# First mixture with one slot for each expert, up to 384 token columns wide, and weights split in halves

## The chip, the core and the metric

The kernel runs on one core of a Trainium2 chip. A core has a matrix engine (PE, with PEld for its weight loads), a vector engine (DVE), a scalar engine (ACT), GpSimd (POOL) and SyncE (SP), which mostly issues DMAs; 16 DMA engines move data between DRAM and the on-chip memories, SBUF and PSUM (8 banks, written by PE). The metric is device time for one execution in microseconds, lower is better.

## The reference

Three layers one after the other, on 1792 tokens of 768 values; what matters here is the second.

```python
# 1. attention: 4 batches, 12 heads, 448 positions, 64 wide, with heads mixed before and after softmax
# 2. first mixture: 8 experts, D = 768, F = 1024; each token goes to one expert
    logits = x @ w_gate
    expert_idx = np.argmax(logits, axis=1)
    ...
    for e in range(E):
        mask = expert_idx == e
        xe = x[mask]
        h = np.maximum(xe @ w1[e], 0.0)
        ye = h @ w2[e]
        out[mask] = gate_w[mask, None] * ye
# 3. second mixture, dense: 768 -> 2048 -> 768
    h = x @ w_in
    r = np.maximum(h, 0.0)
    return ((r * r) @ w_out).astype(np.float32)
```

With the reference's inputs the experts 0 to 7 get 448, 22, 11, 302, 376, 116, 157 and 360 tokens. All are float32; the second mixture's weights come as float64.

## The kernel before

**Precision.** Every float32 operand is split in a high part (fp32r) and the rest, and a product is three matmuls: high by high, high by low, low by high. For a weight tile, `split` (L1021) lets ACT cast the high part (L1042) and DVE, or for a few tiles POOL, subtract the low part (L1043). `ahead` keeps six such tiles made (WB = 6), so a step's tile is made five steps before PE needs it. ACT's and DVE's instructions stand in the order in which the code calls them.

**Router.** During attention, `Router` counts tokens by expert in units of 128 (TM). `early` picks two units for slot 0 before all tokens are known; `table` gives the units of the rest their places, while PE works on slot 0. `side` in `emit_all` steps through this, once per `half` step of slot 0 (PH says at which). After that `ready` is set and the waiting weight reloads and gathers are issued.

**First mixture.** SLOTS has 6 doubles (256 tokens, one expert) and 6 singles (128) in turn, 18 units. A slot loads its expert's w1 (6 tiles of 128 x 1024, `raw1`) and w2 (8 tiles of 128 x 768, `raw2`) by `reload`, on SP's queue, as soon as the slot before has split the same tile. In a double (`double1` L1082, `double2` L1113) the weights are PE's stationary operand and 256 token columns move; the output stands transposed, and `drelu` and `dput` evict it. In a single (`stage1` L1143, `stage2` L1175) the tokens are stationary and 512 or 256 weight columns move; `htrans` and `ytrans` transpose its hidden layer and its result. `xtrans` transposes gathered tokens on PE. The order on PE is pairwise: stage 1 of the double, stage 1 of the single, stage 2 of the double, stage 2 of the single. If a routing needs more units than the 18, `tc.If(more < NT)` runs four more singles and a further piece of the second mixture.

**Conversion.** `convert` turns the float64 w_out to float32 in between: 18 tasks of 7 DVE instructions (`Conv.parts`, L914 to L922), `next(conv)` a part. After a task ACT issues the load of a later one (`conv_load`, into `craw`, CR = 3 buffers), and SP stores the result. `CD` says how many parts follow each step of a double. `compact1` scatters each token's place to DRAM, 16 times, 4 bytes a token (`cid`).

**Second mixture.** `ysplit` makes the operand of 512 tokens, `st1` (L1277) and `st2` (L1316, L1318) alternate for 64 rounds. `open2` opens its pools within the last slot.

Of the kernel before, what the change touches and what calls it, by code (L numbers as in the profile page):

```python
# [7 lines left out]
F32 = mybir.dt.float32  # L8
# [8 lines left out]
DM = H * D  # L17
# [475 lines left out]
QP = QS = 6  # L493
# [9 lines left out]
XK = ((4,6),(3,5))  # L503
CD = (2,2,2,2,2,2),(2,2,2,2,2,2,1,1)
PH = (3,4,5,6,7,8,9,9,10,12,13)
# [3 lines left out]
XS = 3  # L509
HK = 5  # L510
HL = 3
A2 = -1
XD = 12
C0 = 6
W2 = (0,0,1,1,2,2,3,3)
PD = (2,),(2,5)
PS = (2,),(2,5)
# [5 lines left out]
class Router:  # L523

# [51 lines left out]

# [30 lines left out]
    def fill2(self):  # L607
# [4 lines left out]

        self.mate = p.tile([NB, NB], F32, name="mate")
        yield G.memset(self.mate, 1.0)
        yield G.affine_select(out=self.mate, in_=self.mate, compare_op=ALU.is_ge, fill=0.0, base=0,
                              pattern=[[-2, NB // 2], [0, 2]], channel_multiplier=1)
        yield G.affine_select(out=self.mate, in_=self.mate, compare_op=ALU.is_ge, fill=0.0, base=1,
                              pattern=[[2, NB // 2], [0, 2]], channel_multiplier=-1)
# [4 lines left out]
        yield V.tensor_scalar_mul(cst[:, 7:8], cst[:, 6:7], float(TM))  # L623

        self.late = p.tile([UMAX, 1], F32, name="late")
        n = UMAX // 3 - 1
        li = p.tile([UMAX, n], I32, name="li")
        yield G.iota(li, pattern=[[-3, n]], base=0, channel_multiplier=1)
        lt = p.tile([UMAX, n], F32, name="lt")
        yield V.tensor_copy(lt, li)  # L630
        yield V.tensor_scalar(lt[:, 0:1], self.cc[0:UMAX], float(URUN), None, ALU.is_ge)
        yield V.tensor_scalar(lt[:, 1:], lt[:, 1:], 2.0, None, ALU.is_equal)
        yield V.tensor_reduce(self.late, lt, axis=AX.X, op=ALU.max)
# [86 lines left out]
    def units(self, u0, u1, new_ps, tbi):  # L720
# [8 lines left out]
        for z in range(2):  # L729
            nc.tensor.matmul(ps[0:u1, 67 + z:68 + z], lhsT=self.sel[:, z:z + u1], rhs=self.cst[:, 4:5], start=True, stop=True)  # L730
# [4 lines left out]
        V.tensor_copy(tb[:, 0:5], ps[0:u1, 64:69])  # L735
        V.tensor_copy(tbi[:, 0:1], tb[:, 0:1])
        V.scalar_tensor_tensor(out=tb[:, 5:6], in0=tb[:, 4:5], scalar=tb[:, 3:4], in1=self.late[0:u1], op0=ALU.subtract, op1=ALU.mult)
        V.tensor_tensor(out=tb[:, 5:6], in0=tb[:, 5:6], in1=tb[:, 3:4], op=ALU.add)
        V.tensor_tensor(out=tb[:, 6:7], in0=tb[:, 0:1], in1=tb[:, 2:3], op=ALU.add)
        V.scalar_tensor_tensor(out=tbi[:, 2:3], in0=tb[:, 6:7], scalar=tb[:, 5:6], in1=tb[:, 2:3],  # L740
                               op0=ALU.not_equal, op1=ALU.mult)

    def early(self, new_ps):
# [27 lines left out]
        ps = new_ps()  # L771
        nc.tensor.matmul(ps[0:NB, 0:1], lhsT=self.mate, rhs=sel[:, 2:3], start=True, stop=True)
        yield

        V.tensor_scalar(col[:, 2:3], ps[0:NB, 0:1], -1.0, 1.0, ALU.mult, ALU.add)
        yield PE
        yield from self.units(0, EARLY, new_ps, self.tbe)

    def table(self, new_ps):
# [3 lines left out]
        odd, even = cst[:, 5:6], cst[:, 6:7]  # L783
        x = [col[:, i:i + 1] for i in range(16)]
        yield PE
        ps = new_ps()
        self.counts(ps)
        yield

        V.tensor_scalar(x[0], ps[0:NB, 0:1], cst[:, 3:4], None, ALU.subtract)  # L790
        V.tensor_scalar(x[4], x[0], cst[:, 7:8], x[2], ALU.is_gt, ALU.mult)
        V.tensor_tensor(out=x[5], in0=x[4], in1=even, op=ALU.mult)
        V.scalar_tensor_tensor(out=x[6], in0=x[0], scalar=0.0, in1=x[3], op0=ALU.is_gt, op1=ALU.subtract)
        V.tensor_scalar(cst[:, 1:2], x[0], 0.0, float(TM), ALU.max, ALU.min)
        yield PE
        ps = new_ps()
        nc.tensor.matmul(ps[0:NB, 0:1], lhsT=tri, rhs=x[5], start=True, stop=True)
        yield

        V.tensor_scalar(x[7], ps[0:NB, 0:1], odd, None, ALU.subtract)  # L800
        V.tensor_scalar(x[4], x[7], float(QP - 1), x[4], ALU.is_lt, ALU.mult)
        V.tensor_tensor(out=x[5], in0=x[4], in1=even, op=ALU.mult)
        V.tensor_tensor(out=x[6], in0=x[6], in1=x[4], op=ALU.subtract)
        V.tensor_scalar(x[7], x[7], 3.0, odd, ALU.mult, ALU.add)
# [3 lines left out]
        nc.tensor.matmul(ps[0:NB, 1:2], lhsT=ones, rhs=x[5], start=True, stop=True)  # L808
        yield


        Q, fr = x[8], x[9]
        V.tensor_copy(Q, ps[0:NB, 0:1])
        V.tensor_scalar(fr, ps[0:NB, 1:2], -1.0, float(QP - 1), ALU.mult, ALU.add)
        V.scalar_tensor_tensor(out=x[10], in0=Q, scalar=float(QS), in1=fr, op0=ALU.is_ge, op1=ALU.mult)
        V.scalar_tensor_tensor(out=x[11], in0=Q, scalar=-float(QS), in1=fr, op0=ALU.add, op1=ALU.is_lt)
        V.scalar_tensor_tensor(out=x[11], in0=Q, scalar=float(QS), in1=x[11], op0=ALU.is_ge, op1=ALU.mult)
        V.tensor_tensor(out=x[12], in0=Q, in1=fr, op=ALU.subtract)
        V.tensor_scalar(x[12], x[12], 2.0, -2.0 * QP - 1, ALU.mult, ALU.add)
# [105 lines left out]
class Moe:  # L925

    WB, NA = 6, 1

    def __init__(self, tc, ctx, rt, cv, w1, w2, ident, out, slots, main):
# [803 lines left out]
```

## Time and profile before

| | |
|---|---|
| median of 3 runs | 1469.14 us (1465.86 to 1483.52) |
| profiled execution | 1476.49 us, span of its instructions 1474.8 us |
| PE busy | 1383.5 us (94%) |
| DVE busy | 1048.0 us (71%) |
| ACT, POOL busy | 819.7 us (56%), 479.3 us (32%) |
| DMA | 276.49 MB, 187 GB/s in the mean |

A profile shows one execution. "Busy" is the time in which an engine worked on instructions; PE's matmuls overlap, and how fast they follow each other is read from their starts. The chain of waits is followed back from the last instruction: at each step to what released it. A stretch table gives busy time by engine, the granted TensorE clock (PEclk, 1.00 is 2.4 GHz), the DMA engines' busy share and their rate. Times count from the span's start: attention to about 630 us, the first mixture to 987, the second to the end.

### The profile page before, as it was taken

The page shows a single profiled execution, that of the slowest core. Times are in us where ns is not written, and L with a number is a line of the kernel's source. Part 1 is how long each engine was busy: PE and PEld are TensorE (multiplying, and loading weights), DVE is VectorE, ACT ScalarE, POOL GpSimd, SP SyncE. Part 2 cuts the span into 40 slices and gives each one's busy share as a digit, 9 for nine tenths or more (in the row PEclk, how much of TensorE's full clock was granted, in tenths as well). Part 3 has the DMA queues.
Part 4 walks back from the last instruction along what each step waited for, and adds up shares of the span by engine and source line. Part 5 has one row for each costly group of instructions (what it writes and reads, how often), then busy time and mean ns, then how long its engine had stood idle before and what let it go on. Part 6 is the DMA issues. An engine that isn't in the chain of part 4 may idle for free.

```text
span 1474.8 us, 25518 instructions
## 1 busy us (share of the span) xinstructions
PE 1383.5 (94%) x8541; PEld 1182.5 (80%) x8541; DVE 1048.0 (71%) x2331; ACT 819.7 (56%) x1677; POOL 479.3 (32%) x567
## 2 busy tenths in 40 slices
PE   8689998998899989889899999999999999999996
PEld 7468776886678768779788899978888888888896
DVE  4587978897889897789687898889785322423373
ACT  4468775877687767645455666553334323423453
POOL 2234233423352333233343433222223222322343
PEclk7899998999999999999999999999999999999998
DMA  7788778776877674337999998763444333432351
GB/s 156 225 253 244 234 210 247 212 220 190 232 218 218 203 220 130 129 129 190 236 243 226 311 327 284 271 209 129 134 156 147 94 98 96 131 106 86 118 183 56
DMA packets 176474, 276.49 MB, mean 187 GB/s; under 512 B 64143, under 2 KB 125135, under 8 KB 176335
## 3 DMA queue, kind: packets, MB, share of 16 engines
q1 hardware_dynamic: 169915, 255.85, 59.7%
q0 software_dynamic: 3072, 12.59, 2.3%
q10 hardware_dynamic: 3348, 6.33, 1.4%
q8 instruction: 70, 1.15, 0.3%
q14 instruction: 69, 0.57, 0.1%
HBM read 216.85 MB, written 63.51 MB: 190 GB/s over the span
## 4 chain that ended last, share of the span: by engine, by line
PE 66%; DVE 17%; DMA 7%; issue 3%; SPq 3%; ACT 2%; POOL 1%; DVEq 0%; POOLq 0%; ACTq 0%
PE ps L1277 16%; PE psb L1316 10%; PE psb L1122 6%; PE psa L1091 5%; PE po L1318 5%; PE s L190 4%; PE x L268 4%; PE a L234 4%; PE qk L165 3%; DMA r<-in_moe_w_dram 3%; DVE sm L199 3%; DMA vn<-in_v_dram 3%; DVE atl L253 3%; PE psa L1182 2%; PE psb L1150 2%
## 5 line engine op out<-in xcount | busy, mean ns | idle before, releaser
L1043 POOL TENSOR_TENSOR w2l<-r,w2h 128x768 fp32r<-128x768 f32 x88 | 172.8, 1965 | 442.8 <-ACT w2h L1042 405.8
L234 PE MATMUL a<-wr,e 120*128 120x120 f32 (+1 forms) x1440 | 188.5, 278 | 5.9 <-DVE ath L255 4.1
L234 PEld LDWEIGHTS a<-wr,e 120*128 120x128 f32 (+1 forms) x1440 | 178.6, 194 | 16.9 <-POOL wr L225 7.5
L190 PE MATMUL s<-r,wprebd 120*120 120x448 f32 x360 | 172.9, 562 | 19.3 <-ACT e L205 17.8
L1277 PE MATMUL ps<-yb,w1h 128*128 128x512 f32 (+1 forms) x640 | 181.5, 368 | 1.1 <-DVE yb L1264 0.5
L1288 DVE TENSOR_TENSOR room<-room 128x512 f32<-128x512 f32 (+1 forms) x64 | 55.5, 867 | 174.7 <-ACT room L1287 174.6
L165 PE MATMUL qk<-kt,qt 128*120 128x448 f32 (+2 forms) x384 | 171.3, 531 | 5.4 <-DVE qt L107 3.2
L1316 PE MATMUL psb<-w2h,h 128*128 128x512 f32 x448 | 170.3, 396 | 0.0
L1042 ACT CAST w2h<-r 128x768 fp32r<-128x768 f32 x160 | 133.0, 835 | 65.1 <-PE psb L1122 18.6
L1043 DVE TENSOR_TENSOR w1l<-r,w1h 128x768 fp32r<-128x768 f32 (+1 forms) x124 | 143.2, 1165 | 23.9 <-ACT w1h L1042 22.4
L1042 ACT CAST w1h<-r 128x1024 fp32r<-128x1024 f32 (+1 forms) x136 | 128.2, 948 | 57.2 <-DMA r<-in_moe_w_dram 23.6
L205 ACT ACTIVATE e<-s,sm 120x448 f32<-120x448 f32 x180 | 115.1, 640 | 79.2 <-DVE sm L199 78.2
L1287 ACT ACTIVATE room<-ps 128x512 f32<-128x512 f32 (+1 forms) x64 | 35.0, 546 | 209.9 <-PE ps L1277 209.6
L225 POOL TENSOR_SCALAR wr<-wpostbd,sm 120x120 f32<-120x120 f32 x180 | 107.1, 605 | 115.1 <-DVE sm L215 55.0
L199 DVE TENSOR_REDUCE sm<-s 120x1 f32<-120x448 f32 x180 | 112.3, 624 | 37.1 <-PE s L190 32.6
L1277 PEld LDWEIGHTS ps<-yb,w1h 128*128 128x128 f32 x640 | 111.3, 188 | 23.5 <-DVE yb L1265 2.5
L165 PEld LDWEIGHTS qk<-kt,qt 128*120 128x120 f32 (+2 forms) x384 | 69.0, 187 | 72.7 <-issue 46.1
L166 ACT COPY raw<-qk 120x448 f32<-120x448 f32 (+2 forms) x186 | 98.0, 532 | 37.9 <-DMA scr<-raw 24.2
L248 ACT CAST ath<-a 128x480 fp32r<-128x480 f32 x180 | 101.9, 573 | 29.6 <-PE a L234 28.7
L1277 PE MATMUL ps<-yb,w1l 128*128 128x512 f32 (+1 forms) x320 | 117.6, 368 | 0.6 <-DVE w1l L1043 0.6
L1122 PE MATMUL psb<-h,w2h 128*128 128x256 f32 x576 | 107.6, 288 | 0.0
L1318 PE MATMUL po<-w2h,h 128*128 128x256 f32 x384 | 107.1, 279 | 0.0
(328 smaller groups left out, 3227.4 us busy)
## 6 DMA issues: line engine op xcount, KB each, us to landing
r<-in_moe_w_dram SPq DMA_DIRECT2D x72, 512.0 KB
r<-in_moe_w_dram SPq DMA_DIRECT2D x96, 384.0 KB
r<-scr SPq DMA_DIRECT2D x173, 210.0 KB
r<-wi SPq DMA_DIRECT2D x64, 384.0 KB
scr<-raw SPq DMA_DIRECT2D x48, 420.0 KB
r<-wo SPq DMA_DIRECT2D x50, 384.0 KB
craw<-in_moe_w_in_dram SPq DMA_DIRECT2D x32, 384.0 KB
scr<-raw SPq DMA_DIRECT2D x24, 385.0 KB
```

Of the source, the lines that this page charges most:

```text
L165: nc.tensor.matmul(ps[0:n], lhsT=qts[C, h // 2][:, z, h % 2, 0:n], rhs=kts[b, h], start=z == 0, stop=z == 1)
L190: nc.tensor.matmul(ps[0:m], lhsT=const["wpre"][0:m, 0:m], rhs=rts.pop(G)[0:m], start=True, stop=True)
L199: nc.vector.reduce_max(sms[G // 2][0:m, o:o + 1], pss[G][0:m], axis=AX.X, negate=True)
L205: nc.scalar.activation(t[0:m], pss.pop(G)[0:m], AF.Exp, bias=sm[0:m, o:o + 1], accum_out=sm[0:m, 2 + o:3 + o])
L225: nc.gpsimd.tensor_scalar(w.rearrange("p (g i) -> p g i", i=gm), src, sm[0:m, 6 + o:7 + o], None, ALU.mult)
L234: nc.tensor.matmul(o, lhsT=e[0:m, JT[jc]:JT[jc] + JP], rhs=w, start=True, stop=True)
L1042: nc.scalar.copy(hi, raw)
L1043: (nc.gpsimd if on_pool else nc.vector).tensor_tensor(out=lo, in0=raw, in1=hi, op=ALU.subtract)
L1122: self.nc.tensor.matmul(o, lhsT=w[:, ms], rhs=x, start=k == 0 and j == 0 and m % 2 == 0, stop=k == K2 - 1 and j == 2, skip_group_check=True)
L1277: self.nc.tensor.matmul(ps[:, 0:n], lhsT=w[:, ks], rhs=x[:, 0:n], start=k == 0 and m == 0, stop=k == KD - 1 and m == 2)
L1316: self.nc.tensor.matmul(main, lhsT=x[:, ts], rhs=w[:, 0:512], start=f == 0 and m == 0, stop=f == NF - 1 and m == 2)
L1318: self.nc.tensor.matmul(rest, lhsT=x[:, ts], rhs=w[:, 512:768], start=f == 0 and m == 0 and not shared, stop=f == NF - 1 and m == 2, skip_ ...
```

## The change

Slots get widths. `WIDE` gives 9 slots: slot 0 as before with 256 columns, then 384, single, 384, single, 320, single, 192, 192; `table` ranks the experts by what they have left and places them in the slots by `ORDER`, one slot for each; units that don't fit go to the general path, which has nine singles now. A wide slot of over 256 columns (three units) works in two passes: half of the weights' columns at a time, since one output block of 384 columns fills a PSUM bank (`passes`). Weights are therefore split in halves: 512 columns of w1, 384 of w2, six halves ahead. The order on PE is a table (`plan_wide`): first pass of stage 1, the last single's stage 2, second pass, then stage 2's passes around the next single's stage 1. The conversion's parts come two a step in the first stages of the three wide slots and one in their second stages, a few more at the end, and `CR` is 2. The last slot is wide, so `ytrans(last)` behind the first `st1` goes. In the second mixture half of the splits go to a pool of their own (`wu`). Router constants and two small matmuls change with it.

```diff
-URUN = 2 * QP + QS
-SLOTS = [(0, 1)] + [x for u in range(2, URUN - 1, 3) for x in ((u, u + 1), (u + 2,))] + [(URUN - 1,)]
-UMAX = URUN + 4
+WIDE = (2 * TM, 384, 0, 384, 0, 320, 0, 192, 192)
...
+ORDER = (1, 3, 5, 7, 8, 2, 4, 6)
+UMAX = URUN + 9
-CR = 3
+CR = 2
-CD = (2,2,2,2,2,2),(2,2,2,2,2,2,1,1)
-C0 = 6
+C0 = 12
+PG = ((1, 4), (1, 4, 6))
...
+    def passes(self, i):
+        return 2 if self.wide[i] > 256 else 1
+
+    def split(self, w, i, k, z):
+
+        raw, n = (self.raw1, FF // 2) if w == 1 else (self.raw2, DM // 2)
+        t = self.room_w()
+        self.split2((w, i, k, z), raw[k][:, z * n:(z + 1) * n], t[:, 0:n], t[:, 512:512 + n], k in PG[w - 1] and z == k % 2)
+        if z == 0:
+            return
+        if i + 1 < len(self.slots):
+            if self.ready:
+                self.reload(w, i + 1, k)
...
+    def wide1(self, i, k, z, new_ps):
+        n = self.wide[i]
+        per = 2 // self.passes(i)
+        nb = 4 // per
         if k == 0:
-            self.ph[i] = [self.psa() for _ in range(4)]
+            self.ph[i, z] = [new_ps() for _ in range(nb)]
         hi, lo = self.xts[i][k]
-        wh, wl = self.wsp.pop((1, i, k))
-        for m in range(8):
-            o = self.ph[i][m // 2][:, m % 2 * 256:m % 2 * 256 + 256]
+        wh, wl = self.wsp.pop((1, i, k, z))
+        for m in range(4):
+            o = self.ph[i, z][m // per][:, m % per * 256:m % per * 256 + n]
             ms = slice(m * 128, (m + 1) * 128)
             for j, (w, x) in enumerate(((wh, hi), (wh, lo), (wl, hi))):
...
+            prog += [(1, i, 1, X), (2, i, 0, Y), (1, j, 0, X), (2, i, 1, Y)]
...
+            at(2, i, K2 - 1, 0, self.wput, i, 0)
...
+            at(2, i, K2 - 1, 1, self.wput, i, 1)
...
+                elif p % 8 == 0 and spread:
                     rt.compact1(spread.pop(0))
-            if main and p >= K1 + K2 and i < last:
-                for _ in range(CD[w - 1][k] if two else 0):
-                    next(conv, None)
+                if p >= 2 * (K1 + K2):
+                    for _ in range(3 - w if self.passes(i) == 2 else w == z and last - 2 <= i < last):
+                        next(conv, None)
```

On PE, the changed program at the second wide slot (3, L1101 and L1141 are its two stages) and the singles around it (2 and 4; L1171 and L1200 are theirs); L1056 are transposes:

```order
L1101 MATMUL psb<-room,wh 128x384 x72
L1200 MATMUL psa<-wh,h 128x384 x48
L1101 MATMUL psb<-room,wh 128x384 x24
L1056 MATMUL psa<-ident,room 128x128 x6
L1101 MATMUL psb<-room,wh 128x384 x36
L1056 MATMUL psa<-ident,xg 128x128 x6
L1101 MATMUL psb<-room,wh 128x384 x12
L1141 MATMUL psa<-h,wh 128x384 x54
L1056 MATMUL psb<-ident,xg 128x128 x6
L1141 MATMUL psa<-h,wh 128x384 x18
L1171 MATMUL psb<-wh,room 128x512 x12
```

Where 144 matmuls of 256 columns stood at a stretch (L1091, then L1122), a pass is 72 of 384, and single 2's second stage lies between the passes of slot 3's first.

On DVE, the program before, from the last parts of the first conversion task (cw_9211, from craw_8884) on; `w1l` are subtractions of weights, `craw_8915` is the second task's load:

```order
L922 SCALAR_TENSOR_TENSOR cw_9211<-craw_8884,cr_9210 128x384
L914 TENSOR_SCALAR ca_9347<-craw_8915 128x384
L1043 TENSOR_TENSOR w1l_9376<-r1_3_7780,w1h_9375 128x1024
L915 SCALAR_TENSOR_TENSOR ca_9347<-craw_8915,ca_9347 128x384
L916 TENSOR_SCALAR craw_8915<-craw_8915 128x384
L1043 TENSOR_TENSOR w1l_9407<-r1_4_7781,w1h_9406 128x1024
L1109 SCALAR_TENSOR_TENSOR h_9412<-psa_9152,h_9411 128x512
```

On ACT, the program before at the same place; the load that it issues there is craw_9344, the third task's:

```order
L1042 CAST w1h_9320<-r1_2_7779 128x1024
L1076 CAST room_9325<-psb_9327 128x512
L1076 CAST room_9325<-psb_9334 128x256
L904 DMA craw_9344<-in_moe2_w_out_dram 128x768
L1042 CAST w1h_9375<-r1_3_7780 128x1024
```

On DVE, the changed program at the end of the first task (cw_9224, from craw_8890); its loads are named craw again, the second task's is craw_9298:

```order
L904 TENSOR_TENSOR cr_9223<-ca_9222,cr_9223 128x384
L1047 TENSOR_TENSOR wh_9293<-r1_2_7798,wh_9293 128x512
L906 SCALAR_TENSOR_TENSOR cw_9224<-craw_8890,cr_9223 128x384
L898 TENSOR_SCALAR ca_9301<-craw_9298 128x384
L1047 TENSOR_TENSOR wh_9317<-r1_3_7799,wh_9317 128x512
L899 SCALAR_TENSOR_TENSOR ca_9301<-craw_9298,ca_9301 128x384
```

On ACT, the changed program where it issues that load:

```order
L1046 CAST wh_9275<-r1_1_7797 128x512
L1046 CAST wh_9293<-r1_2_7798 128x512
L888 DMA craw_9298<-in_moe2_w_out_dram 128x768
L1046 CAST wh_9317<-r1_3_7799 128x512
L1046 CAST wh_9337<-r1_4_7800 128x512
```

Before, the load issued at the end of a task is read one whole task later; now the load issued behind the cast of wh_9293 is read by the DVE instruction next but one to that tile's subtraction.

## Rows read from the trace of the kernel before

**Rows 1.** Stretches by slot pairs: length, busy PE, PEld, DVE, ACT, POOL, PEclk, DMA, GB/s:

```profile
677.80:740.50 62.70, 56.80 (x400) 53.36 (x399) 48.47 (x73) 33.27 (x43) 23.76 (x19) 0.95 0.93 213
740.50:801.60 61.10, 55.77 (x406) 52.12 (x405) 52.80 (x68) 34.54 (x46) 28.00 (x24) 1.00 0.96 256
801.60:860.20 58.60, 55.49 (x407) 52.03 (x406) 47.05 (x70) 33.95 (x45) 22.35 (x18) 1.00 0.95 295
860.20:914.90 54.70, 54.70 (x407) 52.15 (x406) 47.08 (x68) 34.57 (x46) 17.00 (x10) 1.00 0.86 289
914.90:987.20 72.30, 72.30 (x498) 67.11 (x497) 63.79 (x77) 45.21 (x62) 22.34 (x11) 1.00 0.74 248
```

**Rows 2.** Chain of waits, fourth pair: start us, us, what:

```profile
860.34 8.64 PE psa L1091 x72
...
878.90 8.19 PE psb L1150 x36
...
900.04 0.87 PE psa L1052 x8
...
906.52 8.48 PE psa L1182 x48
```

**Rows 3.** Chain's DMA pieces, 700 to 810 us; the scatters; two stretches:

```profile
701.97 19.87 DMA r<-in_moe_w_dram
...
804.14 12.85 DMA r<-in_moe_w_dram
...
L872 POOL DMA_INDIRECT cid<-tok,cqi x16: 959/1465/1763, 679.8 to 855.0; - x16
...
684.00:692.00 8.00, 8.00 (x69) 8.00 (x69) 7.92 (x12) 3.58 (x5) 3.82 (x3) 1.00 0.92 53
852.00:878.00 26.00, 26.00 (x198) 24.91 (x197) 23.91 (x33) 16.40 (x20) 10.87 (x7) 1.00 0.98 324
```

**Rows 4.** Chain of waits, attention's last products (`av`, 218 columns each):

```profile
616.21 6.34 PE x L268 x56
```

**Rows 5.** Chain of waits at the second mixture's entry:

```profile
988.22 0.35 DVE yb L1264
...
993.71 0.70 DVE room L1265
...
995.18 0.66 PE psb L1052 x6
995.84 4.19 PE ps L1277 x18
1000.03 0.23 PE psb L1316
```

**Rows 6.** DVE's instructions by line: ns min/median/max, first and last start:

```profile
L1043 DVE TENSOR_TENSOR w2l<-r,w2h x66: 941/950/3130, 700.0 to 983.7; 128x768 fp32r<-128x768 f32 x66
L1043 DVE TENSOR_TENSOR w1l<-r,w1h x53: 1206/1217/3417, 678.0 to 961.5; 128x1024 fp32r<-128x1024 f32 x53
...
L917 DVE TENSOR_SCALAR cr<-ca x18: 342/351/2292, 686.0 to 950.4; 128x384 int32<-128x384 int32 x18
L919 DVE SCALAR_TENSOR_TENSOR cr<-craw,cr x18: 541/555/2210, 687.4 to 950.8; 128x384 f32<-128x384 uint32 x18
...
L1109 DVE SCALAR_TENSOR_TENSOR h<-psa,h x24: 673/678/685, 651.4 to 935.2; 128x512 fp32r<-128x512 f32 x24
L1140 DVE COPY yT<-psb x36: 406/410/418, 681.7 to 964.3; 128x256 f32 x36
```

**Rows 7.** A conversion load's issue; its queue, 815.8 to 820.9; gathers' landing:

```profile
815.83 0.33 ACTq L904 DMA_DIRECT2D craw<-in_moe_w_out_dram  x1
...
q10 hardware_dynamic: 141, 0.39, 19.4%
...
DMA to landing us min/median/max: 3.8/6.5/14.0
```

**Rows 8.** The page's head:

```profile
span 1474.8 us, 25518 instructions
```

More of the change, by code (lines that the diff above doesn't have):

```diff
@@ L727, in units @@
         nc.tensor.matmul(ps[0:u1, 64:67], lhsT=self.sel[:, 2:2 + u1], rhs=self.cst[:, 0:3], start=True, stop=True)
[L729 to L730 removed]
+        nc.tensor.matmul(ps[0:u1, 67:68], lhsT=self.sel[:, 1:1 + u1], rhs=self.cst[:, 4:5], start=True, stop=True)
         yield
@@ L929, with __init__ @@
     WB, NA = 6, 1
-    def __init__(self, tc, ctx, rt, cv, w1, w2, ident, out, slots, main):
+    def __init__(self, tc, ctx, rt, cv, w1, w2, ident, out, slots, wide, main):
         self.tc, self.nc, self.ctx, self.slots = tc, tc.nc, ctx, slots
-        self.lastd = max([i for i, x in enumerate(slots) if len(x) == 2], default=-1)
+        self.wide = wide
         self.phase = 1
@@ L998, in psb, with gather @@
         return self.ps_b.tile([128, 512], F32, tag="o", name="psb")
-    def gather(self, u):
-        t = self.xg_p[u % 2].tile([TM, DM], F32, tag="xg", name="xg")
+    def gather(self, i, z):
+        u = self.slots[i][z]
+        if self.main and i == 1 and z == 2:
+            t = self.room("s").bitcast(F32)
+        else:
+            z = z % 2 if self.wide[i] else u % 2 if not self.main else 1
+            t = self.xg_p[z].tile([TM, DM], F32, tag="xg", name="xg")
         self.nc.gpsimd.indirect_dma_start(
@@ new lines, in wrelu @@
+    def wrelu(self, i, z):
+        n = self.wide[i]
+        per = 2 // self.passes(i)
+        if z == 0:
+            self.hts[i] = []
+        room = 4 if n <= 192 else 2
+        for b, ps in enumerate(self.ph.pop((i, z))):
+            m = len(self.hts[i])
+            if m % room == 0:
+                self.hroom = [self.hidden(tag, i < len(self.slots) - 1)[:, 0:room * n].rearrange("p (k t) -> p k t", t=n)
+                              for tag in ("gh", "gl")]
+            hi, lo = [h[:, m % room:m % room + per] for h in self.hroom]
+            src = ps[:, 0:per * 256].rearrange("p (k t) -> p k t", k=per)[:, :, 0:n] if per == 2 else ps[:, 0:n].unsqueeze(1)
+            self.nc.scalar.activation(hi, src, AF.Relu)
+            self.nc.vector.scalar_tensor_tensor(out=lo, in0=src, scalar=0.0, in1=hi, op0=ALU.max, op1=ALU.subtract)
+            self.hts[i] += [(hi[:, a], lo[:, a]) for a in range(per)]
+        if z == 1:
+            self.xts.pop(i)
@@ L1120, in double2, with wide2 @@
+    def wide2(self, i, k, z, new_ps):
+        n = self.wide[i]
+        if k == 0 and (z == 0 or self.passes(i) == 2):
+            self.py[i, z] = [new_ps() for _ in range(3)]
+        per = 2 // self.passes(i)
+        py = self.py[i, z if per == 1 else 0]
+        hi, lo = self.hts[i][k]
+        wh, wl = self.wsp.pop((2, i, k, z))
+        for m in range(3):
+            a = m + 3 * z * (per - 1)
+            o = py[a // per][:, a % per * 256:a % per * 256 + n]
             ms = slice(m * 128, (m + 1) * 128)
@@ L1383, in run @@
                     self.reload(w, 0, k)
-            self.gather(slots[0][0])
-            self.gather(slots[1][0])
+            self.gather(0, 0)
+            self.gather(1, 0)
         if main:
@@ L1390, in run @@
         if not main:
-            self.xtrans(0)
+            self.xtrans(0, 0)
         conv = self.convert()
-        def fetch(i):
-            for u in slots[i] if i <= last else ():
-                if self.ready:
-                    self.gather(u)
-                else:
-                    self.waiting.append(u)
         halves = iter(range(2 * (K1 + K2)))
@@ L1489, in run @@
             if i == 0:
-                self.ytrans(last)
+                if not main:
+                    self.ytrans(last)
                 for _ in conv:
@@ L1650, in side @@
                 next(table)
-                yield from at(PH[6])
-                next(table)
-                yield from at(PH[7])
                 ps = moe.pst()
@@ L1656, in side @@
                 next(part)
+                yield from at(PH[6])
+                next(part)
+                yield from at(PH[7])
+                next(table)
                 yield from at(PH[8])
-                next(part)
-                next(table)
-                yield from at(PH[9])
-                next(table)
-                yield from at(PH[10])
                 for _ in table:
```

459 lines of the change are left out of this document (223 added, 236 removed).

## Prediction

> **What bounds the kernel now.** I read the split of the program into stretches first. The first mixture's matmuls run from 630 us to 987 us; from 677.8 us, behind slot 0, the stretch table has one row for each pair of a double and a single slot [rows 1]. PE is busy for 295.1 of these 309.4 us and DVE for 259.2 (sums of the five rows), so two engines are close together, and a term that leaves PE can come back on DVE.
>
> Then the chain of waits over the one pair without a stall [rows 2]. It is PE alone: a double's 144 matmuls of 256 columns per stage go out every 120 ns (8.64 us for 72), the single's 36 of 512 columns every 227.5 ns, its 48 of second stage in 8.48 us, transposes every 109 ns (0.87 us for 8). Two stages of 144 x 0.120, 8.19, 8.48 and 32 transposes give 54.7 us, the pair's whole length. So the other pairs, 62.7, 61.1 and 58.6 us long, hold 8.0 + 6.4 + 3.9 = 18.3 us of stalls; the last row is 54.7 plus one more single (17.6).
>
> What stalls them: the chain there shows waits for weight loads from DRAM, 19.87 and 12.85 us the longest [rows 3]. They end where the 16 scatters of 4-byte places (compact1) end, 855 us. Behind the first scatter the DMA engines are 92% occupied and move 53 GB/s; without them 324 GB/s [rows 3].
>
> **Part 1: PE's work.** The reference's inputs send 448, 376, 360, 302, 157, 116, 22 and 11 tokens to the experts; slot 0 takes 256 of the 448 early, and the rest (192) and the others fit the widths 384, 384, 320, 192, 192 and three times 128. So the general path stays empty, and the main path has 9 slots where it had 12. Spacing: 384 columns lie between the rows at 256 (120 ns) and 512 (227.5): by a straight line 174 ns, for 320 columns 147. For 192 columns no row exists; the nearest is attention's product with 218 columns, 56 in 6.34 us, 113 ns each [rows 4]; transposes of 128 columns are at 109. A matmul with its own weight load thus does not fall under 109 to 113 ns, and I take 112 for 192.
>
> The Trainium skill, TensorE: Matmul & The Clock Gate, section Back-to-back issue gap, gives an isolated matmul N/2.4 + 2.5 ns: 82.5 ns for 192 columns. By it the two 192-wide slots would be 17 us shorter. The row at 218 columns, for which it gives 93 ns, measures 113, so I keep the row.
>
> A wide slot has 288 matmuls: 50.1 us at 384, 42.3 at 320, 32.3 at 192. A single's second stage is now 48 of 384 columns, 8.34 us for 8.48. The pairs in the new order, with their transposes: slots 1 and 2 70.1 us (32 transposes), 3 and 4 70.7 (38), 5 and 6 62.3 (32), 7 and 8 66.5 (576 x 0.112 and 18). Sum 269.6 against 309.4: 39.8 us less, of which 18.3 are the old stalls and 21.5 work. Slot 0 keeps its 288 matmuls and router and gets 6 more transposes: +0.6.
>
> **Part 2: entry of the second mixture.** Before, the chain from 988.2 to 994.4 us runs through DVE, which makes yb (ysplit) behind its other work, and PE then transposes the last single's y [rows 5]: 36 matmuls and 6 transposes take from 987.0 to 1000.0, 13.0 us, where 36 take 8.4. Now the last slot is wide: no y transposes, and ysplit's six steps lie in stage-2 steps of 2.0 us (18 x 0.112) for 1.1 us of DVE work each (0.35 and 0.70). I take the 4.6 us off.
>
> So without any new stall: -39.8 + 0.6 - 4.6 = -43.8 us.
>
> **Part 3: weights in halves.** Each split is two halves: 28 casts and 28 subtractions a slot. The DRAM bytes are 9 x 6.29 MB for 12 x 6.29, so a pair moves about 17.5 MB (weights 12.6, conversion 3.4, gathers 1.6) in 71 us, 247 GB/s, where the clean pair moved 289 [rows 1]. A raw tile is now free only when both halves are split, but from there to the next slot's use lie 15 to 20 us of PE work, by the steps' order; 3.1 MB at 247 GB/s take 12.7. So I price left-over DMA waits at 2 us in all (bounds: none, and the 18.3 of before).
>
> DVE's work for a pair, from medians [rows 6]: a subtraction is 1.217 us at 1024 and 0.950 at 768, so 0.683 at 512 and 0.549 at 384; a conversion part 0.468 in the mean (three at 0.351, four at 0.555); copies of 256 columns 0.410, so 0.276 at 128. The same prices give 47.5 us for the clean pair of before (11 x 1.217 + 12 x 0.950 + 25 x 0.468 + 4 x 0.678 + 6 x 0.410 + 5.8 for evicted transposes), measured 47.1: they hold. Now: 20 x 0.683 + 26 x 0.549 = 27.9; conversion 40 x 0.468 = 18.7, since its 126 parts lie in three wide slots instead of five doubles; relu 8 x 0.545 = 4.4; wput 18 x 0.276 = 5.0; transposes 6.9. Together 62.9 of 70.1 to 70.7 us (89%, was 86%), and about 61.2 of 62.3 in the third pair (98%). POOL's part gets smaller (two halves of 512 and three of 384 a slot for one 1024 and two 768).
>
> **Part 4: the conversion's loads, the late thing.** With CR 3, two loads are out before the first task and each task's end issues the load for the task after next. With CR 2 one is out, and a task's end issues the load that the next task reads at once: in the order, DVE's read of craw_9298 stands right behind the previous task's last part, and ACT issues that load one cast earlier. 17 loads of 393 KB are so placed. Such a load took 5.1 us in a quick stretch (issued at 815.83, its 0.39 MB through by 820.9), and a gather of the same size 3.8 to 14.0 us, median 6.5 [rows 7]. Queued behind the waiting part on DVE: the subtractions that PE needs, the relu and wput evictions. What covers it: PE has five split halves in hand, 5 x 12 x 0.174 = 10.4 us in a wide first stage, 7.8 in a second; and ACT, which runs as far ahead as the rooms let it, issues the next load earlier once DVE lags. So DVE should settle at a lag of about 5.5 us, unseen in wide passes. But a single's steps are 0.69 and 0.52 us, five of them 3.0 us in the mean, and DVE's own work in a single's pass exceeds PE's: in the first stage 5 x 0.683 + 5 x 0.549 + wput 2.5 + evicted transposes 1.1 = 9.7 for PE's 8.9, in the second 8 x 0.549 + 5 x 0.683 + relu 2.2 = 10.0 for 8.3; 1.2 us in the mean. Price at each entry from a wide pass to a single's: 5.5 - 3.0 + 1.2 = 3.7 us. There are five such entries with conversion before them: 18.5 us. The third pair has no DVE slack to catch up: 2 us. With the DMA's 2 the new stalls are 23 us (bounds: none; and every load exposed, second rival).
>
> **Sum.** -43.8 + 23 = -20.8 us. The profiled execution took 1476.5 us (span 1474.8 [rows 8]) and lies 7.4 above the median, 1469.1. 1476.5 - 20.8 = 1455.7, or 1448 against the median.
>
> **Rivals.**
> *DVE absorbs the loads.* If ACT is always far enough ahead, stalls stay under 14 us, and the time falls to 1426 to 1440; with 6 us it is 1431. For it: the clean pair kept PE full with DVE at 86%. Against it: the third pair, and zero head start.
> *The loads are exposed: slower.* Place: DVE's first part of each task. If ACT reaches the issue only when DVE reaches the read, each load costs w us of DVE time: 5.7 w a pair, less the slack of 7.2, 7.8 and 1.1. The stalls are 17 w - 16. The gain is gone from w = 3.5; at 5.5 they are 78 us and the time is 1503. For it: the order, and that DVE waits in line. Against: it needs ACT never ahead, while PE's rooms allow it five steps.
> *192 columns are cheap.* If spacing went on falling under 256 columns in proportion (90 ns), 576 x 22 ns = 13 us less: 1435. By the Trainium skill's formula above the gain would be 17 us. Against: 113 at 218 columns.
> *The change does not do what it says:* one token over a width sends units into the general path, at least a single slot's 16.5 us each and a second mixture: above 1600. Width 192 is filled exactly, but the routing leaves no token near expert 0's border.
>
> **Chances.** Forecast (stalls 14 to 50) 0.57, absorbed 0.27, 192 cheap 0.03, exposed 0.11, general path 0.02. A step of 2% (29 us: 1440 and 1498), about what a measurement of this kernel can tell from no change, is passed downwards by the absorbed and cheap cases, 0.30, and upwards by most of the exposed case, 0.08. Range 1432 to 1475: it leaves out the best of the absorbed case and most of the exposed one. The forecast's own range is 1440 to 1475.
>
> **What would show it.** Right: the wide first stages at 174 ns, 192 columns at 109 to 115; DVE idle ahead of the first conversion part with a load as releaser; PE waiting on subtractions within singles; first mixture's end near 972; entry under 10 us. Wrong: DVE's waits for loads many times 5 us, PE idle within wide passes too, or no wait for a load at all; or PE waiting for weight loads as before.

## The result and the profile after

The changed kernel takes 1489.63 us (median of 20 runs, 1483.04 to 1500.62); the kernel before, in 20 runs, 1475.58. The ratio is 1.0105, 95% interval 1.0086 to 1.0124: 14 us slower by the medians, where 20.8 us less were forecast. Between the two profiled executions it is 16.7 us (1474.8 to 1491.5). Where they lie, by PE's matmuls (for the stretches behind slot 0, each gap between two matmul starts is split into the normal spacing of its shape, and what is over it; what is over it in stretches at half clock counts as clock up to one more spacing, the rest as idle; 1.4 and 1.5 us of small differences in spacing stand in no row):

| us | before | after | forecast of the difference | measured |
|---|---|---|---|---|
| up to the first mixture | 630.2 | 632.2 | 0 | +2.0 |
| slot 0 | 47.6 | 52.1 | +0.6 | +4.5 |
| behind slot 0: work | 287.2 | 266.4 | -21.5 | -20.8 |
| behind slot 0: PE idle | 18.6 | 41.5 | (old stalls off 18.3, new ones 23:) +4.7 | +22.9 |
| behind slot 0: lost at half clock | 2.0 | 13.3 | none | +11.3 |
| second mixture, to the end | 487.8 | 484.5 | -4.6 | -3.3 |

The stretch table (length, busy PE, PEld, DVE, ACT, POOL, PEclk, DMA share, GB/s) of the changed kernel, from slot 1's first matmul to the second mixture's; it answers to [rows 1]:

```profile
684.30:757.20 72.90, 66.14 (x359) 63.09 (x358) 51.23 (x105) 33.36 (x63) 19.65 (x22) 0.95 0.68 163
757.20:845.20 88.00, 76.84 (x412) 72.92 (x411) 60.35 (x128) 41.39 (x81) 24.07 (x29) 0.94 0.78 200
845.20:930.30 85.10, 70.78 (x406) 65.36 (x405) 57.58 (x125) 39.97 (x78) 27.70 (x24) 0.92 0.72 227
930.30:1007.10 76.80, 75.70 (x644) 74.60 (x644) 54.33 (x102) 43.76 (x86) 17.38 (x14) 1.00 0.64 203
```

A stretch holds a single's second stage one pair later than the forecast counted it, so by the forecast's work they would last 61.8, 70.7, 62.3 and 74.8 us. The last, where only four parts of the last conversion task are left and no load is waited for, is 2 us over that; the first three are 11, 17 and 23 over, with the clock at 0.92 to 0.95. DVE is busy for 68 to 70% there, not 89: it waits too. What for, its two longest waits say, and one of ACT's that bears on them (us in total, times, longest):

```profile
DVE ca L898 <- DMA craw<-in_moe_w_out_dram: 52.2, 10, 8.4
ACT wh L1046 <- PE psb L1101: 42.4, 34, 4.0
DVE wh L1047 <- ACT wh L1046: 30.2, 39, 2.3
```

The chain of waits goes through these loads again and again, and it shows the new shapes' spacing (start us, us, what):

```profile
703.48 9.55 DMA craw<-in_moe_w_out_dram
...
751.09 9.70 DMA craw<-in_moe_w_out_dram
...
789.56 6.24 PE psb L1101 x36
...
841.17 9.13 DMA craw<-in_moe_w_out_dram
...
877.40 1.77 PE psb L1101 x12
...
975.00 16.08 PE psa L1141 x144
```

36 matmuls of 384 columns in 6.24 us are 173 ns each, 12 of 320 in 1.77 are 148, 144 of 192 in 16.08 are 112.

How a load comes late is seen on two engines. DVE's row at 706.35 is the last before the wait; ACT had issued the load at 703.48 (timeline: start us, us, what, in brackets the idle time before it and what ended it):

```profile
705.88 0.56 DVE L906 SCALAR_TENSOR_TENSOR cw<-craw,cr 128x384 f32<-128x384 int32 x1
706.35 0.55 DVE L1047 TENSOR_TENSOR wh<-r,wh 128x384 fp32r<-128x384 f32 x1
713.15 0.58 DVE L898 TENSOR_SCALAR ca<-craw 128x384 int32<-128x384 int32 x1 [6.25 <-DMA craw<-in_moe_w_out_dram]
```

```profile
703.40 0.52 ACT L1046 CAST wh<-r 128x384 fp32r<-128x384 f32 x1 [1.08 <-PE psb L1101]
703.48 0.34 ACTq L888 DMA_DIRECT2D craw<-in_moe_w_out_dram  x1
705.52 0.51 ACT L1046 CAST wh<-r 128x384 fp32r<-128x384 f32 x1 [1.61 <-PE psb L1101]
707.61 0.51 ACT L1046 CAST wh<-r 128x384 fp32r<-128x384 f32 x1 [1.58 <-PE psb L1101]
709.64 0.51 ACT L1046 CAST wh<-r 128x384 fp32r<-128x384 f32 x1 [1.51 <-PE psb L1101]
712.16 0.59 ACT L1083 CAST room<-psa 128x512 fp32r<-128x512 f32 x1 [2.01 <-PE psa L1056]
712.46 0.34 ACTq L888 DMA_DIRECT2D craw<-in_moe_w_out_dram  x1
```

ACT is not free to run ahead: its rooms (the buffers for split halves) are full, so each cast waits until PE has used a room, every 2 us, and the load goes out 3 us before DVE wants it and lands over 9 us after its issue. Only while DVE stands still does ACT gain on it: the next load is out at 712.46, before DVE has begun the task ahead of it. By the rows of all 17 loads, five were issued before DVE had begun the task ahead, and none of these was waited for; of the other twelve, ten were.

A stall is paid twice. PE stands for 2.3 us from 809.1, and the granted clock is at half (1.2 GHz) from 811.5 on (stretches, columns as above):

```profile
808.50:811.50 3.00, 0.73 (x5) 0.41 (x4) 1.01 (x3) 0.62 (x1) 0.00 (x0) 1.00 0.07 10
811.50:814.90 3.40, 3.40 (x14) 3.30 (x14) 3.37 (x8) 0.13 (x1) 0.00 (x0) 0.50 0.00 0
814.90:818.00 3.10, 3.10 (x20) 3.10 (x19) 3.10 (x5) 2.60 (x5) 2.13 (x2) 1.00 0.73 257
```

Behind slot 0 there are eight such pieces, seven of 3.4 us and one of 6.8, and 13.3 us are lost in them. Before, there was one.

### The profile page after: what moved, and what is told of

Read it like the earlier page. It is cut to its first block, busy times and chain, and to the rows that moved or that the text cites. A ratio compares the mean times of both kernels' runs of the same rounds, so it can differ in the third digit from the quotient of the medians.

```text
span 1491.5 us, 25077 instructions
## 1 busy us (share of the span) xinstructions
PE 1375.9 (92%) x8241; PEld 1182.5 (79%) x8241; DVE 1003.2 (67%) x2439; ACT 797.4 (53%) x1764; POOL 454.8 (30%) x596
## 4 chain that ended last, share of the span: by engine, by line
PE 63%; DVE 17%; DMA 9%; issue 4%; SPq 2%; ACT 2%; POOL 1%; DVEq 0%; POOLq 0%; ACTq 0%
PE ps L1295 15%; PE psb L1334 10%; PE s L190 5%; PE po L1336 5%; PE x L268 4%; PE a L234 4%; DMA craw<-in_moe_w_out_dram 4%; PE psa L1141 3%; PE qk L165 3%; DVE sm L199 3%; PE psb L1101 3%; DMA vn<-in_v_dram 3%; DVE atl L253 2%; PE psb L1141 2%; DVE wh L1047 2%
## 5 line engine op out<-in xcount | busy, mean ns | idle before, releaser
L1046 ACT CAST wh<-r 128x384 fp32r<-128x384 f32 (+2 forms) x315 | 187.7, 615 | 159.1 <-PE psb L1101 42.4
L1047 DVE TENSOR_TENSOR wh<-r,wh 128x512 fp32r<-128x512 f32 (+2 forms) x249 | 173.8, 717 | 38.1 <-ACT wh L1046 34.0
L1047 POOL TENSOR_TENSOR wh<-r,wh 128x384 fp32r<-128x384 f32 (+2 forms) x66 | 100.1, 1517 | 317.2 <-ACT wh L1046 302.3
L1334 PE MATMUL psb<-wu,h 128*128 128x512 f32 x450 | 160.3, 395 | 0.0
L1047 POOL TENSOR_TENSOR wu<-r,wu 128x768 fp32r<-128x768 f32 x43 | 82.6, 1920 | 216.3 <-ACT wu L1046 216.3
L199 DVE TENSOR_REDUCE sm<-s 120x1 f32<-120x448 f32 x180 | 112.3, 624 | 38.5 <-PE s L190 34.0
L1295 PE MATMUL ps<-yb,wh 128*128 128x512 f32 (+1 forms) x630 | 135.5, 366 | 0.2 <-DVE wh L1047 0.2
L165 PEld LDWEIGHTS qk<-kt,qt 128*120 128x120 f32 (+2 forms) x384 | 69.1, 188 | 74.6 <-issue 46.5
L1295 PEld LDWEIGHTS ps<-yb,wh 128*128 128x128 f32 x630 | 105.7, 188 | 20.7 <-DVE wh L1047 0.4
L1141 PE MATMUL psa<-h,wh 128*128 128x384 f32 (+2 forms) x576 | 97.0, 326 | 16.1 <-DVE room L1084 9.6
L1336 PE MATMUL po<-wu,h 128*128 128x256 f32 x384 | 107.5, 280 | 0.0
L1141 PEld LDWEIGHTS psa<-h,wh 128*128 128x128 f32 x576 | 91.9, 198 | 18.1 <-DVE room L1084 10.5
```

The source lines that it names most:

```text
L165: nc.tensor.matmul(ps[0:n], lhsT=qts[C, h // 2][:, z, h % 2, 0:n], rhs=kts[b, h], start=z == 0, stop=z == 1)
L199: nc.vector.reduce_max(sms[G // 2][0:m, o:o + 1], pss[G][0:m], axis=AX.X, negate=True)
L1046: self.nc.scalar.copy(hi, raw)
L1047: (self.nc.gpsimd if on_pool else self.nc.vector).tensor_tensor(out=lo, in0=raw, in1=hi, op=ALU.subtract)
L1141: self.nc.tensor.matmul(o, lhsT=w[:, ms], rhs=x, start=k == 0 and j == 0 and a % per == 0, stop=k == K2 - 1 and j == 2, skip_group_check=True)
L1295: self.nc.tensor.matmul(ps[:, 0:n], lhsT=w[:, ks], rhs=x[:, 0:n], start=k == 0 and m == 0, stop=k == KD - 1 and m == 2)
```

## The experiments

All ratios are against the kernel before on the same chip, with their 95% intervals; the other columns are from each run's profile, behind slot 0 unless it says slot 0.

| kernel | ratio | slot 0 | length behind it | PE idle | lost at half clock |
|---|---|---|---|---|---|
| before | 1 | 47.6 | 309.2 | 18.6 | 2.0 |
| the change | 1.0105 (1.0086 to 1.0124) | 52.1 | 322.7 | 41.5 | 13.3 |
| lead3 | 0.9974 (0.9943 to 1.0005) | 52.5 | 309.7 | 32.3 | 9.4 |
| lead6 | 0.9893 (0.9861 to 0.9926) | 52.5 | 296.6 | 24.9 | 3.6 |
| before_cr2 | 1.0237 (1.0192 to 1.0282) | 48.3 | 344.8 | 45.4 | 11.1 |
| after_scat | 0.9949 (0.9926 to 0.9972) | 52.5 | 301.2 | 28.1 | 5.2 |
| before_scat | 0.9840 (0.9797 to 0.9884) | 48.5 | 290.2 | 1.7 | 0.0 |
| lead6_scat | 0.9836 (0.9796 to 0.9875) | 52.4 | 284.3 | 16.3 | 0.0 |
| zs_early | 1.0114 (1.0076 to 1.0152) | 49.8 | 333.0 | 48.3 | 16.6 |
| lead6_zs | 0.9887 (0.9830 to 0.9945) | 46.0 | 297.9 | 24.9 | 5.1 |
| best_m0 | 0.9828 (0.9801 to 0.9856) | 47.2 | 286.0 | 16.4 | 1.5 |
| best_m2 | 0.9823 (0.9796 to 0.9851) | 49.8 | 284.1 | 14.7 | 1.5 |
| before_best | 0.9832 (0.9805 to 0.9860) | 43.6 | 290.2 | 1.7 | 0.0 |
| pool_more | 0.9844 (0.9810 to 0.9878) | 48.0 | 290.4 | 18.3 | 4.3 |

**The loads' lead.** With two buffers, the one that a load needs is free as soon as the task before last has ended, so the load can go out anywhere in the task before its own: behind its first part (lead6) or, with 3 for 0, behind its fourth (lead3):

```diff
-            yield from cv.parts((kind, f, z), cw, a, r)
-            self.conv_load(self.nc.scalar)
+            for m, part in enumerate(cv.parts((kind, f, z), cw, a, r)):
+                if m == 0:
+                    self.conv_load(self.nc.scalar)
+                yield part
```

> The changed kernel, but each conversion load is issued behind the first of the seven parts of the task before it, not behind the last; nothing else differs. Theory A (the loads come late): the trace of the changed kernel has 52 us of DVE waiting for these loads within the first mixture; a lead of six parts is about 6 us in a wide first stage and 10 us in a second, and loads take 3 to 9 us from issue to landing, so the waits fall under 12 us, PE's idle time behind slot 0 from 41 to about 12 us, its time at the low clock from 13 to about 4, and the kernel's time to about 1452 us (1442 to 1462). Theory B (DVE is too full, whatever the loads do): the waits for loads go, waits for subtractions take their place, and the time stays over 1478 us. Theory C (the earlier issue makes ACT wait for DVE, since the buffer is the one that the task before last has just left): ACT waits over 20 us at the load's line and the time is 1475 to 1495 us.

> The changed kernel, but each conversion load is issued behind the fourth of the seven parts of the task before it: half the lead of the run beside it. Theory A: about 3 us of lead in a first stage, 5 in a second, so of the 52 us of waits some 20 to 25 are left; the time lies between the changed kernel and the run with the full lead, near 1468 us (1458 to 1476). Theory B: over 1480 us for both. Theory C: as the full lead or faster, since ACT waits less.

The waits for the loads, in lead3 and then in lead6:

```profile
DVE ca L898 <- DMA craw<-in_moe_w_out_dram: 29.4, 8, 9.8
```

```profile
ACT wh L1046 <- DVE ca L898: 20.2, 5, 6.0
...
DVE ca L898 <- DMA craw<-in_moe_w_out_dram: 7.6, 3, 5.4
```

From 52.2 us of waits to 29.4 and 7.6, and from 1.0105 to 0.9974 and 0.9893: the time follows the lead. Theory A holds and B falls. A was too hopeful on what is left: 24.9 us of idle time where 12 were expected, and 29.4 us of waits in lead3 where 20 to 25 were. C is there in part: ACT waits 20.2 us at the load's line.

**Two buffers alone.** `CR = 2` in the kernel before:

> The kernel before with two conversion buffers for three, its order otherwise the same: this part of the change alone. Theory A: each load is then issued at the end of a task and read at once, as in the changed kernel; with DVE 86% busy in a pair and 17 loads of 4 to 9 us, DVE waits over 30 us, PE's idle time behind slot 0 rises from 19 to about 40 us, and the time from 1475.6 to about 1497 us (1485 to 1520). Theory B (the exposed loads matter only where DVE is 89 to 98% busy): within 8 us of the kernel before.

```profile
DVE ca L914 <- DMA craw<-in_moe_w_out_dram: 69.5, 12, 16.9
```

2.4% slower, 35 us, and 35.6 us more behind slot 0. So it is this line of the change, without any width or half, that costs; and it costs at a DVE of 86% too. The changed kernel with three buffers was not run.

**The scatters.** The 16 scatters go behind the first mixture, in the kernel before (where the first condition has 5 for 8) and in the changed one:

```diff
-                elif p % 8 == 0 and spread:
+                elif p % 8 == 0 and False:
...
-            if main and i == 6:
+            if main and i < 8:
+                for _ in range(2):
+                    rt.compact1(spread.pop(0))
+            if main and i == 12:
                 rt.compact2(self.c_p)
```

> The kernel before with the same move of the 16 scatters behind the first mixture. The prediction held that its 18.3 us of stalls in the pairs come from weight loads that the scatters slow. If so, PE's idle time behind slot 0 falls from 18.6 to under 5 us and the time by 13 to 20 us, 0.9 to 1.4%. If the stalls come from the amount of weights (12 slots of 6.3 MB) and not from the scatters, the time moves by under 5 us.

> The changed kernel, but the 16 scatters of token places go out in the first eight rounds of the second mixture, two a round, and the read of the places follows in round 12; nothing else differs. Theory F (the scatters slow every queue, so the conversion's loads land 8 to 9 us after issue where quick ones take 3 to 4): the loads land within 3 to 5 us, DVE's 52 us of waits for them fall to about 25, PE's idle time behind slot 0 from 41 to about 22 and its time at the low clock from 13 to about 6, and the time by 20 to 28 us to about 1.6% below the changed kernel. Theory G (it is the missing lead alone that costs, and the DMA engines have room): the time moves by less than 8 us.

Of the kernel before nothing but 1.7 us of idle time is left, and it gains 1.6% (23 us, where 13 to 20 were expected): the forecast's reading of [rows 3] was right. Its clock, too, is full (stretch behind slot 0, columns as above):

```profile
681.90:972.10 290.20, 290.20 (x2108) 274.91 (x2107) 255.58 (x353) 182.24 (x238) 88.06 (x46) 1.00 0.81 275
```

The changed kernel gains as much (0.0156), theory F; by the ends of the packets in the ACT queue its loads now take 2.7 to 7.3 us from issue, where 5 of 17 took 8 to 9 us. Theory F had hoped for more: landing within 3 to 5 us, 25 us of waits and 22 of idle time. DVE still waits for the loads, and PE is idle for 28.1 us:

```profile
DVE ca L898 <- DMA craw<-in_moe_w_out_dram: 34.4, 9, 6.1
```

So the scatters had two victims: before, the weight loads, and now the conversion's loads. And with scatters gone from both, the change is again 1.1% the slower one (0.9949 to 0.9840).

> The changed kernel with the conversion's loads issued six parts earlier and the scatters behind the first mixture. With the longer lead alone, PE is idle for 24.9 us behind slot 0 and loses 3.6 us at the low clock; the chain of waits there shows weight loads of 17 and 14 us and a conversion load of 12 us. If the scatters cause these: idle under 12 us, the first mixture behind slot 0 near 280 us for 296.6, time 12 to 18 us below the run with the lead alone. If what is left is DVE's own work in the singles' passes: idle over 20 us, time within 5 us of it.

Both moves together: the same time as before_scat. The 16.3 us of idle time missed the expectation of under 12, and the time, 8 us below lead6, that of 12 to 18; of this, about 4 us (2.3 idle, 1.6 at half clock) are a wait in the second mixture at 1030 us, for a weight load behind the scatters (chain of waits):

```profile
1013.14 18.65 DMA r<-wi
```

The scatters slow what they lie beside there as well.

**The held copy.** In the router's part of slot 0, DVE copies 27 x 120 values, and this took 6.0 us; beside it POOL (changed kernel):

```profile
661.22 2.29 POOL L1412 MEMSET yT<- 128x1280 f32 x2
663.45 1.00 POOL L1047 TENSOR_TENSOR wh<-r,wh 128x384 fp32r<-128x384 f32 x1
664.38 2.28 POOL L1412 MEMSET yT<- 128x1280 f32 x2
```

```profile
660.53 0.26 DVE L833 COPY big<-psa 27x112 f32<-27x112 f32 x1 [0.23 <-PE psa L830]
660.72 6.00 DVE L835 COPY big<-tb 27x120 f32<-27x120 f32 x1
```

The copy ends when POOL's row of three ends, 666.7 us. The experiment calls the clearings earlier:

```diff
-ZS = (12,14,16,18,20,22)
+ZS = (2,3,4,5,6,7)
```

> The changed kernel, but the six clearings of yT by POOL are called five to fifteen half steps earlier in slot 0, ahead of POOL's gathers. In the trace a DVE copy of 27 x 120 values (big from tb) lasts 6.0 us and ends with POOL's second clearing, 666.7 us; before the change it lasted 5.1 us and ended with POOL's last clearing too. Theory D (DVE's copy is held by POOL's work beside it): the copy falls under 1 us, slot 0 shortens from 52.1 to about 47 us, the time by 4 to 6 us to about 1484. Theory E (the copy is slow by its own operand, repeated 120 times): it stays at 5 to 6 us and the time the same within 2 us.

> The changed kernel with the conversion's loads issued six parts earlier and POOL's six clearings of yT ahead of its gathers. On the changed kernel alone the same move shortened the held DVE copy from 6.0 to 0.2 us and slot 0 by 2.3 us, and the time not measurably, behind slot 0 the loads' stalls moved. With these mostly gone the 2.3 us should show: 1.5 to 4 us below the run with the lead alone. If the time of the first mixture behind slot 0 is set by something that doesn't start with slot 0's end (a transfer that lands when it lands), it is the same as with the lead alone.

In zs_early the copy takes 0.20 us: DVE was held, theory D. But slot 0 is only 2.3 us shorter, not 5, because the hold has moved. The clearings now stand beside an earlier step of the router, which takes 0.23 us in the changed kernel; it ends with the fifth of them, and PE waits 3.9 us behind it:

```profile
644.60 5.58 POOL L1412 MEMSET yT<- 128x1280 f32 x5
644.80 5.42 DVE L773 TENSOR_SCALAR t<-eoh,col 112x8 f32<-112x8 f32 x1
```

The time is no shorter: behind slot 0 that execution lost 10 us more in the same stalls. In lead6_zs the same step takes 0.99 us beside the same five clearings, slot 0 is 6.5 us shorter in the profile, and the time within the interval of lead6's. What it is worth in time is not settled by these runs.

**All together.** The loads' lead, the early clearings, and the scatters put eight in the last slot (every third step) and one in each of the second mixture's rounds 0 to 7; on the scatters as a diff (best_m0; best_m2 has 2 for 0 in the lead's line); and the kernel before with the scatters of before_scat and the clearings of zs_early:

```diff
-                elif p % 8 == 0 and spread:
+                elif i == last and p % 3 == 0 and len(spread) > 8:
                     rt.compact1(spread.pop(0))
...
-            if main and i == 6:
+            if main and spread:
+                rt.compact1(spread.pop(0))
+            if main and i == 12:
                 rt.compact2(self.c_p)
```

> The changed kernel with three things moved: the conversion's loads issued behind the first part of the task before (lead of six parts), POOL's clearings of yT ahead of its gathers, and the scatters placed eight in the last slot (one every third step) and one a round in rounds 0 to 7 of the second mixture, read back in round 12. The run with the longer lead and the scatters two a round was at 0.9836 of the kernel before, with slot 0 at 52.4 us, 284.3 us behind it, and a wait of some 4 us for a weight load in the second mixture at 1030 us, behind the scatters. Expected: slot 0 near 47 us, 282 to 288 behind it, no such wait: 7 to 10 us less, a ratio of 0.976 to 0.980. If clearings moved earlier or scatters in the last slot cost elsewhere what they save here, the ratio stays within 0.003 of 0.9836.

> The same with the loads issued behind the third part (lead of four). With the lead of six ACT waited 11.8 us at the load's line for DVE's first part of a task; without scatters a load lands 2.7 to 6.8 us after issue, and four parts are 4 us in a first stage, 6 in a second. Theory H (ACT's wait there delays casts and so PE): the waits at that line fall under 4 us, PE's idle time behind slot 0 from 16.3 to about 12, 2 to 4 us faster than the lead of six. Theory I (DVE's own work in the singles' passes sets what is left): the same within 2 us; DVE's waits for loads come back with 5 to 10 us in all.

> The kernel before with the same two moves that have nothing to do with the widths: the scatters behind the first mixture (two a round, rounds 0 to 7) and the clearings of yT ahead of the gathers. It shows what the widths are worth once nothing stalls either kernel. Scatters alone gave 0.984; the held copy of 5.1 us in slot 0 should fall to 0.2 and take 3 to 5 us off: 0.981 to 0.982. The widths' 20.8 us of saved PE work then show as 3 to 8 us between this kernel and the two beside it if the singles' passes stay short of DVE, and as 12 to 20 us if they don't.

best_m2 beats both kernels: 1.8% below the one before, 2.8% below the change. The ratio of 0.976 to 0.980 that was expected of best_m0 is missed. And before_best is level with the two: neither 3 to 8 us nor 12 to 20 show between them. The widths still save their 21 us of PE work, and 284.1 us behind slot 0 against 290.2 are what is left of them; slot 0 costs them 6.2 in best_m2, where the router's step of zs_early is held for 5.42 us again, and 3.6 in best_m0, where it takes 2.09. The comparison is not quite even: before_best has the scatters two a round, and its second mixture takes 492.6 us, 487.8 in the kernel before; a weight load of 19 us stands in its chain of waits there, as in lead6_scat. The kernel before with the scatters placed as in best_m0 was not run. What takes the rest of the widths' gain is seen in best_m2's waits:

```profile
PEld psb L1171 <- DVE wh L1047: 7.0, 9, 1.3
...
PEld psa L1101 <- DVE room L1084: 3.8, 1, 3.8
PEld psa L1200 <- DVE wh L1047: 3.7, 5, 1.3
```

7.0 and 3.7 us of the 14.7 are in the singles' two stages, behind DVE's subtractions; 3.8 at slot 1's start. Lead four is no faster than lead six, as theory I has it. But the signs in the trace, ACT's wait under 4 us for H and DVE's waits for loads back with 5 to 10 us for I, both failed: the first is 10.8 us, the second 1.1. So H was not put to the test.

```profile
ACT wh L1046 <- DVE ca L898: 10.8, 4, 6.8
```

Last, on top of best_m2, POOL was given more of the subtractions:

```diff
-        ..., k in PG[w - 1] and z == k % 2)
+        ..., k in PG[w - 1])
```

> The run with the lead of four parts, clearings early and scatters at the end of the first mixture, and POOL subtracting both halves of its five weight tiles a slot and not one half of each: ten of 28 halves for five. There PE is idle for 14.7 us behind slot 0, of it 3.7 at slot 1's first step behind the router's last work on DVE, and about 10 in the singles' passes waiting for DVE's subtractions. Theory I (DVE's own work in the singles' passes): five halves a slot are 3 us of DVE time, 6 a pair; the waits in the singles fall by 5 to 8 us and the time by 4 to 8 us. Theory K (POOL is too slow there, 1.0 to 1.3 us a half against steps of 0.52 and 0.69 us, and its work holds DVE's instructions beside it): PE's waits only change their releaser, from DVE's to POOL's subtractions, and the time is the same or up to 8 us more.

POOL's busy time behind slot 0 rises from 74.6 to 122.9 us, and DVE's hardly falls (230.5 to 228.1), though 41 instructions left it (best_m2, then pool_more):

```profile
682.10:966.20 284.10, 274.87 (x1815) 264.82 (x1814) 230.48 (x462) 158.22 (x308) 74.58 (x70) 0.99 0.74 229
681.70:972.10 290.40, 277.57 (x1813) 267.56 (x1814) 228.09 (x421) 158.07 (x308) 122.91 (x109) 0.98 0.71 222
```

```profile
PEld psb L1171 <- DVE wh L1047: 7.4, 6, 2.4
...
PEld psa L1200 <- DVE wh L1047: 5.1, 4, 2.8
```

Theory K, by its second half: the time is the same within the interval, PE still waits for DVE, not for POOL, and DVE is slower. What DVE's instructions took over their medians grew from 21.7 to about 40 us. Two rows of pool_more show how:

```profile
831.91 1.16 POOL L1047 TENSOR_TENSOR wh<-r,wh 128x384 fp32r<-128x384 f32 x1 [4.29 <-ACT wh L1046]
832.10 1.38 DVE L1047 TENSOR_TENSOR wh<-r,wh 128x384 fp32r<-128x384 f32 x1
```

A subtraction of 384 columns takes DVE 552 ns where POOL does nothing. One that begins while POOL subtracts ends 0.41 to 0.42 us behind POOL's, up to 1.38 us in all (14 of the 15 that began with over 0.2 us of POOL's left); one that was under way when POOL's began takes 0.54 to 0.56 us (14 of 15).

## Why the prediction was wrong

**Right.** What bounds the kernel before, and the scatters as the cause of its stalls (before_scat). PE's work: -20.8 for -21.5, with 173 ns at 384 columns (174 forecast), 147 at 320 (147), 112 at 192 (112). The rival of cheap 192 columns falls. For an isolated matmul of that width the formula of the Trainium skill (TensorE: Matmul & The Clock Gate, Back-to-back issue gap) gives an estimate of 82.5 ns; the measurement decides for the 112 of the row. The entry of the second mixture: its first 36 matmuls take 8.24 us where they took 13.0 with the transposes, so the 4.6 us are gone; 1.3 come back later in that mixture.

```profile
1007.16 8.24 PE ps L1295 x36
```

PE waits for subtractions within singles, and DVE idles ahead of the first conversion part, as the last part of the forecast named it. Two of its signs of being wrong came as well: waits for loads of over 5 us (seven of the ten), and PE idle within wide passes.

**Wrong: part 4, the price of the loads.** The order showed that a load is issued at the end of the task before its own, and the forecast said so; then it covered this with two statements that fail. First, that ACT runs as far ahead as its rooms let it and issues earlier once DVE lags. ACT's rooms are full in a wide pass, and PE's use of a room paces it; it gains on DVE only while DVE already stands. A stall spares at most the next two loads (the three longest did), and then the waits come back. Second, that the lag settles at 5.5 us and stays unseen in wide passes. About 25 of the 41.5 us of idle time are in wide passes (the gaps behind L1101 and L1141 up to 930 us). So the step that failed is this price: the sum had 18.5 us for the loads, 23 of new stalls in all, and the runs showed the second rival, the exposed loads. DVE waits 52.2 us for 17 loads, w = 3.1, and by the rival's formula 17 w - 16 = 36 us of stalls; 41.5 were measured, and before_cr2 shows that two buffers by themselves cost the kernel before 35 us. The rival's chance of 0.11 was the misjudgment; the zero head start, read from the order, should have weighed more than an engine's room to run ahead, which the wait rows of before did not show.

**Wrong: the clock is missing from the sum.** No term priced what a stall does to the clock: 13.3 us. The rows of before held the hint (PEclk 0.95 in the stretch with the longest stalls, [rows 1]). With the rival's 36 us of stalls alone the sum is 1476.5 - 43.8 + 36 = 1469, still a gain. The profiled execution took 1493; of the 24.5 us between, the clock is 11.3 (13.3 for 2.0), stalls over the formula 5.2, slot 0 3.9, and the stretch before the first mixture, the rest of the second and PE's work 4.

**Wrong: DMA, 2 us.** The old stalls of 18.3 us were taken off and 2 put back, since fewer weight bytes flow, though the forecast itself had laid those stalls to the scatters. The scatters stayed in the first mixture and now delay the conversion's loads: moving them gives the changed kernel 23 us. The two causes overlap: of 54.8 us (idle and clock) the lead alone takes 26.3, the scatters alone 21.5, both 38.5.

**Wrong: slot 0, +0.6.** It is +4.5. Nine slots of the general path for four make the clearings of yT larger (2.29 us for a pair where five took 2.93), and they hold DVE's copy in slot 0, on the path: 6.0 us for 5.1. That is about 1 us. PE's idle time in slot 0 is 10.5 us for 7.0; the rest of that is waits for other steps of the router, which stand in other half steps now and were not tried one by one.

**DVE in the singles.** That DVE's work exceeds PE's there was right, at 1.2 us a pass; for the six passes of the three singles that is 7.2 us. With loads and scatters out of the way 14.7 to 16.4 us of idle time are left; in best_m2 10.7 us of waits are in the singles' stages and 3.8 at slot 1's start, behind the router. DVE's whole work was priced a little high: it was busy for 60.4 and 57.6 us in the second and third stretch, for 62.9 and 61.2 in the sum.

## What to carry to other kernels

A double buffer is worth only the lead that its load gets: put the load where its buffer comes free, not where the loop ends, and when an order shows a load issued right ahead of its reader, price it as exposed unless a wait row shows the issuing engine idle for another reason. Price a stall of PE with the clock that it loses behind it. Before a kernel gets less work, look for what stalls it: moving 16 small scatters brought the kernel before 1.6%, and the change at its best, with its scatters moved too, has 1.8%. When work is moved out of the way of a held instruction, look at what stands beside its new place.

## What was not expected of the hardware

A DVE copy of 27 x 120 values takes 0.20 us alone, and 6.0 where POOL works at the same time, to the end of three POOL instructions in a row. The router's step of 0.23 us (L773) took 0.99, 2.09 and 5.42 us beside the same five clearings (lead6_zs, best_m0, zs_early): to the end of the first, the second and the fifth. The Trainium skill (SBUF — State Buffer, Who interferes with whom) says that DVE and GpSimd share one pair of ports as an exclusive lock, that copies can take both, and that a DVE instruction with two SBUF inputs contends with a GpSimd instruction that reads SBUF. The traces agree, with 0.20 and 6.0 us for the copy, and 0.55 and up to 1.38 us for the subtraction beside POOL's; that work given to POOL saved DVE nothing is what it comes to here.

Sixteen scatters of 4 bytes a token cost either kernel 23 us in the first mixture, though they move 7 KB in all.
